# Moving the transposes of a routed-attention and MoE kernel from TensorE to the DMA crossbar

## The chip, the cores and the metric

The kernel runs on one core of a Trainium2 chip. The metric is the device time of one execution in microseconds (us), median of the timed runs. A run more than 1.5% above the fastest of its kernel is put down as slow and is left out of every ratio.

A ratio below is the mean time of one kernel's fast runs over the mean time of the fast runs of the kernel before in the same rounds on the same chip, with a 95% interval. It is therefore not quite the ratio of the medians that stand beside it.

## The reference

Four batches of eight heads, 768 tokens, head size 64. Each token of q and k is assigned to the nearest of 16 centroids of its head, a token attends only to tokens with its own centroid, and the attention output goes through a two-layer block with h·cos(h) between the layers.

```python
q_assign = argmax(einsum('bhsd,hcd->bhsc', q_n, c_n), -1)      # q_n, k_n, c_n: normalised
k_assign = argmax(einsum('bhsd,hcd->bhsc', k_n, c_n), -1)
mask = q_assign[:, :, :, None] == k_assign[:, :, None, :]
scores = where(mask, q @ k.T / sqrt(D), -1e9)
x = (softmax(scores) @ v)  ->  (3072, 512)
h = x @ w_in               # 512 -> 2048
out = (h * cos(h)) @ w_out # 2048 -> 512
```

## The kernel before

Heads are taken in pairs, sixteen pairs in all, four to a batch. For each pair, q and k are scaled and split into an fp16 high part and an fp16 low part, side by side in a staging tile `stg`. TensorE transposes the tile, the centroid matmuls and a row maximum give the one-hot assignment, and the transposed one-hots are put as 16 extra rows under the 64 rows of q and k. Then one matmul with 80 rows of depth gives score plus mask at once.

```python
stg[p] = op_pool.tile([P, 2, 2, NT, 2, D], FP16, name="stg")      # op_pool: 2 buffers
...
def tr(p, hh, a, act=False):                     # four a pair
    trp = ps_one.tile([P, NT, P], FP16, name="one")
    for t in range(NT):                          # NT = 6
        nc.tensor.transpose(out=trp[:, t, :], in_=st[:, a, hh, t]..., identity=ident)
    xT = op_pool.tile([P, S], FP16, name=f"qkT{a}{hh}", bufs=3)
    nc.vector.tensor_copy(out=xT, in_=trp...)
    qkT[p, a, hh] = xT
...
def ot(p):                                       # one-hots of the pair
    for t in range(NT):
        nc.tensor.transpose(out=tro[:, t, :], in_=oh[:, t], identity=ident)
    nc.vector.tensor_scalar(out=ohT, in0=tro..., scalar1=oh_mul, scalar2=oh_add, ...)
    for hh in range(2):
        for a in range(2):                       # to partitions 64..79 of qkT
            nc.sync.dma_start(out=qkT[p, a, hh][D:KDIM, :], in_=ohT[r0:r0 + NCL])
...
def e_chunk(p, c):                               # scores, then exp
    nc.scalar.activation(out=e_flat[...], in_=ps, func=AF.Exp, scale=1.0 / SUNIT)
...
def g_tr(p):                                     # attention output -> xt, for the MoE matmuls
    for t in range(NT):
        nc.tensor.transpose(out=trx[:, t, :], in_=st[:, t], identity=ident)
    nc.vector.tensor_copy(out=xt_of[b][:, hp, :], in_=trx...)
...
# stage s: scores of pair s, with as fillers: centroids and one-hots of s+1,
# attention-times-v and x transpose of s-1, splits and transposes of s+2, output matmuls
# SyncE issues all loads of q, k, v, the one-hot copies and the stores, in order.
```

After every fourth pair comes an MoE block (the two-layer block of the reference), which reads the transposed x of the batch. The kernel puts TensorE's results into PSUM tiles; the copy from there is called an evacuation below (63 of the 64 copies of transposed q and k are by VectorE, 551 ns each).

The softmax here doesn't subtract the row's maximum and nothing guards it: scores larger than these inputs give would overflow.

## Time and profile before

| quantity of the kernel before | value |
|---|---|
| median time | 373.2 us |
| span of the profiled run | 373.6 us |
| TensorE busy | 336.1 us, 90% |
| VectorE, ScalarE busy | 230.2 us, 210.1 us |
| traffic | 31.42 MB |
| start to the first MoE block | 96.73 us |

The prediction below shows the lines of the page and reads them. The granted clock (PEclk) is the share of full speed at which TensorE was allowed to run. The DMA share is the mean busy share of the 16 DMA engines. The run that was profiled (375.4 us) is put down as slow, 1.5% above the fastest run of this kernel on any chip of the study (369.7 us), so its stage lengths may be about 1% long.

For the sections that follow I cut every profile at the same marks: the moments at which ScalarE loads its cosine table (an MoE block begins) and its exponential table (attention begins again), ACT_TABLE_LOAD in the trace, 1.28 us each. This gives eight stages.

### The profile page before, as it was taken

Reading aid. Unit: us, or ns where it says so; the run is one execution under the profiler, and the core shown is the slowest. Engines: PE = TensorE matmul, PEld = TensorE weight load, DVE = VectorE, ACT = ScalarE, POOL = GpSimd, SP = SyncE. Lnnn points to the kernel's source line nnn. Section 1 sums busy time; section 2 is a strip of 40 time slices with the busy share of each in tenths; the row PEclk is TensorE's granted clock in tenths of the full one; section 3 lists DMA queues with packets and bytes.
Section 4 is the critical chain, followed back from the end, with each engine's and each line's share of the span. In section 5 each row is a group of like instructions: output and inputs, shape, how many; then the busy total and the mean of one; then the engine's idle time right before and its main releaser. Section 6 shows DMA issues by size and latency. Waiting matters only on the chain.

```text
span 373.6 us, 8520 instructions
## 1 busy us (share of the span) xinstructions
PE 336.1 (90%) x3656; PEld 242.6 (65%) x3656; DVE 230.2 (62%) x438; ACT 210.1 (56%) x205; POOL 28.1 (8%) x64
## 2 busy tenths in 40 slices
PE   0596569779999899999999899999998999999995
PEld 0465357566887567766977666769875666676662
DVE  5779266784765678777555767866656442354451
ACT  3163367557644677777434686786446888243320
POOL 4610021010000001100100000110000000000000
PEclk9998598895899999999999899999999999999999
DMA  7999295432420022542210110100000000101002
GB/s 230 341 241 267 77 187 150 136 104 88 147 71 28 30 80 98 145 138 78 89 44 29 36 35 12 39 31 12 2 29 30 25 29 28 58 2 56 31 28 84
DMA packets 21334, 31.42 MB, mean 84 GB/s; under 512 B 2416, under 2 KB 17712, under 8 KB 21296
## 3 DMA queue, kind: packets, MB, share of 16 engines
q1 hardware_dynamic: 18608, 26.68, 21.7%
q0 software_dynamic: 2688, 4.19, 6.3%
q8 instruction: 28, 0.46, 0.5%
q14 instruction: 10, 0.08, 0.1%
HBM read 27.30 MB, written 6.29 MB: 90 GB/s over the span
## 4 chain that ended last, share of the span: by engine, by line
PE 76%; ACT 10%; DMA 7%; DVE 4%; issue 1%; SPq 1%; ACTq 0%; DVEq 0%
PE one L316 22%; PE big L297 21%; PE big L246 16%; PE one L264 8%; ACT e_ring L252 7%; PE one L175 6%; DMA qkT<-ohT 6%; ACT cos_t L303 2%; DMA qk_nat<-in_q_dram 2%; PE one L282 2%; PE one L190 1%; ACT L252 1%; DVE g L304 1%; PE one L213 1%; DVE stg L167 1%
## 5 line engine op out<-in xcount | busy, mean ns | idle before, releaser
L252 ACT ACTIVATE e_ring<-big 128x1024 f16<-128x1024 f32 x144 | 143.1, 1023 | 62.4 <-PE big L246 61.3
L246 PE MATMUL big<-qkT,qkT 80*128 80x512 f16 (+1 forms) x384 | 96.6, 357 | 19.3 <-DMA qkT<-ohT 12.1
L303 ACT ACTIVATE cos_t<-big,bias_pi 128x1024 f16<-128x1024 f32 x48 | 53.5, 1114 | 77.1 <-PE big L297 77.0
L316 PE MATMUL one<-w_out_sb,g 128*128 128x512 f16 x384 | 96.3, 379 | 0.0
L297 PE MATMUL big<-xt,w_in_sb 128*128 128x256 f16 x768 | 92.1, 272 | 0.1
L304 DVE TENSOR_TENSOR g<-big,cos_t 128x1024 f16<-128x1024 f32 x48 | 58.7, 1223 | 52.5 <-ACT cos_t L303 52.5
L297 PEld LDWEIGHTS <-w_in_sb 128*128 128x128 f16 x768 | 74.2, 98 | 15.8 <-issue 0.2
L246 PEld LDWEIGHTS <-qkT 80*128 80x128 f16 x384 | 35.2, 104 | 43.2 <-DMA qkT<-ohT 12.6
L316 PEld LDWEIGHTS <-g 128*128 128x128 f16 x384 | 37.1, 98 | 32.9 <-issue 0.8
L264 PEld LDWEIGHTS <-e_ring 128*128 128x128 f16 x1152 | 48.2, 101 | 8.3 <-issue 2.9
L264 PE MATMUL one<-v_ext,e_ring 128*128 128x65 f16 x1152 | 51.2, 199 | 0.0
L321 DVE COPY o_sb<-one 128x512 f32<-128x512 f32 x24 | 16.6, 690 | 35.4 <-PE one L316 35.4
L155 POOL CAST v_ext<-v_nat 128x384 f16<-128x384 f32 x32 | 20.1, 637 | 222.8 <-PE one L264 169.3
L181 DVE COPY qkT<-one 128x768 f16<-128x768 f16 x63 | 32.2, 551 | 6.6 <-PE one L175 5.8
L167 DVE SCALAR_TENSOR_TENSOR stg<-qk_nat,stg 128x384 f16<-128x384 f32 x64 | 33.9, 553 | 0.1
L175 PE MATMUL one<-ident,stg 128*128 128x128 f16 x384 | 32.4, 246 | 0.0
L175 PEld LDWEIGHTS <-stg 128*128 128x128 f16 x384 | 28.8, 112 | 3.4 <-issue 1.6
L271 DVE RECIPROCAL recip<-one 128x6 f32<-128x6 f32 x32 | 6.2, 194 | 28.1 <-PE one L264 27.9
L166 DVE TENSOR_SCALAR stg<-qk_nat 128x384 f16<-128x384 f32 x64 | 21.1, 358 | 2.2 <-DMA qk_nat<-in_k_dram 1.2
L197 DVE TENSOR_REDUCE csum<-one 128x192 f32<-128x384 f32 x32 | 16.7, 552 | 6.0 <-PE one L190 5.7
L272 DVE TENSOR_TENSOR av_stage<-one,recip 128x384 f16<-128x384 f32 x32 | 17.8, 555 | 0.7
L190 PE MATMUL one<-cside,qkT 128*128 128x32 f16 x384 | 14.4, 178 | 2.2 <-DVE qkT L181 1.9
(45 smaller groups left out, 109.8 us busy)
## 6 DMA issues: line engine op xcount, KB each, us to landing
v_nat<-in_v_dram SPq DMA_DIRECT2D x16, 384.0 KB, 4.8
out_dram<-o_sb SPq DMA_DIRECT2D x24, 256.0 KB, 2.0
qk_nat<-in_q_dram SPq DMA_DIRECT2D x15, 384.0 KB, 3.4
qk_nat<-in_k_dram SPq DMA_DIRECT2D x15, 384.0 KB, 3.8
w_in_sb<-in_moe_w_in_dram POOLq DMA_DIRECT2D x4, 512.0 KB, 10.3
w_out_sb<-in_moe_w_out_dram POOLq DMA_DIRECT2D x4, 512.0 KB, 12.3
qkT<-ohT SPq DMA_DIRECT2D x60, 24.0 KB, 1.9
qk_nat<-in_q_dram SPq DMA_DIRECT2D x2, 192.0 KB, 3.0
```

The source lines that it names most:

```text
L155: nc.gpsimd.tensor_copy(out=v_bufs[(2 * p + hh) % NV][:, :, 0:D], in_=v_nat[:, hh])
L166: nc.vector.tensor_scalar_mul(dst[:, :, 0, :], src, ASCALE)
L167: nc.vector.scalar_tensor_tensor(out=dst[:, :, 1, :], in0=src, scalar=ASCALE, in1=dst[:, :, 0, :], op0=ALU.mult, op1=ALU.subtract)
L175: nc.tensor.transpose(out=trp[:, t, :], in_=st[:, a, hh, t].rearrange("p c d -> p (c d)"), identity=ident)
L181: nc.vector.tensor_copy(out=xT, in_=trp.rearrange("p t q -> p (t q)"))
L246: nc.tensor.matmul(ps[:, x:x + n], lhsT=qkT[p, 1, hh][0:KDIM, jt * P:(jt + 1) * P], rhs=qkT[p, 0, hh][0:KDIM, col:col + n], start=True, st ...
L252: nc.scalar.activation(out=e_flat[:, base + c * CW:base + (c + 1) * CW], in_=ps, func=AF.Exp, scale=1.0 / SUNIT)
L264: nc.tensor.matmul(av[:, i, :], lhsT=e_ring[:, r + j, i * P:(i + 1) * P], rhs=vx[:, j, :], start=(j == 0), stop=(j == NT - 1))
L297: nc.tensor.matmul(ps[:, fi, :], lhsT=w_in_sb[:, ft, (f0 + fi) * P:(f0 + fi + 1) * P], rhs=xt_of[b][:, ft, cols], start=(ft == 0), stop=(f ...
L303: nc.scalar.activation(out=cos_t, in_=ps, func=AF.Sin, bias=bias_pi2, scale=1.0)
L304: nc.vector.tensor_tensor(out=g[:, f0:f0 + FQ, :], in0=ps, in1=cos_t, op=ALU.mult)
L316: nc.tensor.matmul(ops, lhsT=g[:, f, i * P:(i + 1) * P], rhs=w_out_sb[:, f, :], start=(f == 0), stop=(f == NFPT - 1))
```

## The change

The intent is to take 546 transposes away from TensorE, the engine that bounds the kernel (busy 336.1 of 373.6 us), and their evacuations away from VectorE. From pair 1 on a DMA transposes the whole staging tile (`dma_start_transpose` in the program, DMA_TRANSPOSE in the traces; crossbar transpose in the texts). The one-hots are then written over the low parts of that tile, and a second crossbar transpose brings q, k and the one-hots into place together. The attention output goes through the crossbar as well. The mask's constant moves into the bias of the exponential, and the weights are loaded from the second pair on.

```diff
+    def tr_dma(p, second=False):
+        xT = op_pool.tile([P, 2, 2, NT, P], FP16, name="xT2" if second else "xT1", bufs=2)
+        nc.sync.dma_start_transpose(
+            out=xT.rearrange("p a h t q -> p (a h t) q"),
+            in_=stg[p].rearrange("p a h t c d -> p (a h t c d)"))
+        ... qkT[p, a, hh] = xT[:, a, hh]
 ...
-    def ot(p): ...
+        for a, val in ((0, 1.0), (1, GAP)):                  # in c_post, p >= 1
+            dst = stg[p][:, a, :, :, 1, 0:NCL]
+            nc.vector.tensor_tensor(out=dst, in0=cs_of[p][:, :, a], in1=..., op=ALU.is_ge)
+            if a:
+                nc.vector.tensor_scalar_mul(dst, dst, GAP)
 ...
-                             func=AF.Exp, scale=1.0 / SUNIT)
+                             func=AF.Exp, scale=1.0 / SUNIT, bias=bias_gap)
 ...                                                         # g_tr
-        for t in range(NT):
-            nc.tensor.transpose(out=trx[:, t, :], in_=st[:, t], identity=ident)
-        nc.vector.tensor_copy(out=xt_of[b][:, hp, :], in_=trx...)
+        nc.sync.dma_start_transpose(out=xt_of[b][:, hp].rearrange("p (t q) -> p t q", t=NT), in_=st)
 ...
-        r.append((34, lambda hh=hh, a=a: tr(p, hh, a)))       # tr_list
+        r = [(8, lambda hh=hh, a=a: split(p, hh, a)) for hh in range(2) for a in range(2)]
+        return r + [(1, lambda: tr_dma(p))]
 ...
-        return [(34, lambda: ot(p))]
+        return [(1, lambda: tr_dma(p, True))]
 ...
-                if weight_jobs:
+                if s >= 1 and weight_jobs:
```

More of the change, by code (lines that the diff above doesn't have):

```diff
@@ L76 @@
     bias_pi2 = consts.tile([P, 1], FP32, name="bias_pi2")
-    oh_mul = consts.tile([P, 1], FP32, name="oh_mul")
-    oh_add = consts.tile([P, 1], FP32, name="oh_add")
+    bias_gap = consts.tile([P, 1], FP32, name="bias_gap")
     warm = consts.tile([1, 1], FP32, name="warm")
-    NV, NOH = 8, 2
+    NV = 8
     v_bufs = [consts.tile([P, NT, DE], FP16, name=f"v_ext{i}") for i in range(NV)]
-    oh_bufs = [consts.tile([P, NT, 2, 2, 2 * NCL], FP16, name=f"oh{i}") for i in range(NOH)]
+    oh_buf = consts.tile([P, NT, 2, 2, 2 * NCL], FP16, name="oh")
     NE = 4
@@ L176, in tr @@
                                 identity=ident)
-        xT = op_pool.tile([P, S], FP16, name=f"qkT{a}{hh}", bufs=3)
+        xT = op_pool.tile([P, S], FP16, name=f"qkT{a}{hh}", bufs=1)
         if act:
@@ L182, in tr @@
         qkT[p, a, hh] = xT
+    def tr_dma(p, second=False):
[3 more added lines that the diff above has]
+            in_=stg[p].rearrange("p a h t c d -> p (a h t c d)"))
+        for a in range(2):
+            for hh in range(2):
+                qkT[p, a, hh] = xT[:, a, hh].rearrange("p t q -> p (t q)")
     def c_mm(p, hh, a):
@@ L204, in c_post @@
         nc.vector.reduce_max(out=r, in_=cs, axis=AX.X)
-        oh = oh_bufs[p % NOH].rearrange("p t h a c -> p (h a) t c")
-        nc.vector.tensor_tensor(out=oh[:, 2 * h0:2 * (h0 + n), :, 0:NCL], in0=cs,
-                                in1=r.to_broadcast([P, 2 * n, NT, NCL]), op=ALU.is_ge)
-    def ot(p):
-        oh = oh_bufs[p % NOH].rearrange("p t h a c -> p t (h a c)")
-        tro = ps_one.tile([P, NT, P], FP16, name="one")
-        for t in range(NT):
-            nc.tensor.transpose(out=tro[:, t, :], in_=oh[:, t], identity=ident)
-        ohT = small_pool.tile([P, S], FP16, name="ohT")
-        nc.vector.tensor_scalar(out=ohT, in0=tro.rearrange("p t q -> p (t q)"),
-                                scalar1=oh_mul, scalar2=oh_add, op0=ALU.mult, op1=ALU.add)
-        for hh in range(2):
-            for a in range(2):
-                r0 = (2 * hh + a) * 2 * NCL
-                nc.sync.dma_start(out=qkT[p, a, hh][D:KDIM, :], in_=ohT[r0:r0 + NCL])
+        if p == 0:
+            oh = oh_buf.rearrange("p t h a c -> p (h a) t c")
+            nc.vector.tensor_tensor(out=oh[:, 2 * h0:2 * (h0 + n), :, 0:NCL], in0=cs,
+                                    in1=r.to_broadcast([P, 2 * n, NT, NCL]), op=ALU.is_ge)
+            return
+        for a, val in ((0, 1.0), (1, GAP)):
+            dst = stg[p][:, a, :, :, 1, 0:NCL]
+            nc.vector.tensor_tensor(
+                out=dst, in0=cs_of[p][:, :, a],
+                in1=r.rearrange("p (h a) t o -> p h a t o", a=2)[:, :, a].to_broadcast([P, 2, NT, NCL]),
+                op=ALU.is_ge)
+            if a:
+                nc.vector.tensor_scalar_mul(dst, dst, GAP)
     def ot_head(p, hh):
-        oh = oh_bufs[p % NOH].rearrange("p t h a c -> p t h (a c)")
+        oh = oh_buf.rearrange("p t h a c -> p t h (a c)")
         n = 4 * NCL
@@ L230, in ot_head @@
         if hh == 0:
-            nc.scalar.mul(qkT[p, 0, hh][D:KDIM, :], tf[0:NCL], -GAP)
+            nc.scalar.copy(qkT[p, 0, hh][D:KDIM, :], tf[0:NCL])
         else:
-            nc.vector.tensor_scalar_mul(qkT[p, 0, hh][D:KDIM, :], tf[0:NCL], -GAP)
-        nc.vector.tensor_scalar(out=qkT[p, 1, hh][D:KDIM, :], in0=tf[2 * NCL:3 * NCL],
-                                scalar1=-1.0, scalar2=1.0, op0=ALU.mult, op1=ALU.add)
+            nc.vector.tensor_copy(out=qkT[p, 0, hh][D:KDIM, :], in_=tf[0:NCL])
+        nc.vector.tensor_scalar_mul(qkT[p, 1, hh][D:KDIM, :], tf[2 * NCL:3 * NCL], GAP)
     def e_chunk(p, c):
@@ L278, in g_tr @@
             xt_of[b] = xt_pool.tile([P, HPB, S], FP16, name="xt")
-        trx = ps_one.tile([P, NT, P], FP16, name="one")
-        st = av_of.pop(p).rearrange("p t h d -> p t (h d)")
-        for t in range(NT):
-            nc.tensor.transpose(out=trx[:, t, :], in_=st[:, t], identity=ident)
-        nc.vector.tensor_copy(out=xt_of[b][:, hp, :], in_=trx.rearrange("p t q -> p (t q)"))
+        st = av_of.pop(p).rearrange("p t h d -> p (t h d)")
+        nc.sync.dma_start_transpose(out=xt_of[b][:, hp].rearrange("p (t q) -> p t q", t=NT), in_=st)
     g_of = {}
@@ L328, in g_list @@
     def g_list(p):
-        return [(34, lambda: g_tr(p))]
+        return [(1, lambda: g_tr(p))]
     def tr_list(p):
-        r = []
-        for hh in range(2):
-            for a in range(2):
-                r.append((0, lambda hh=hh, a=a: split(p, hh, a)))
-                r.append((34, lambda hh=hh, a=a: tr(p, hh, a)))
-        return r
+        r = [(8, lambda hh=hh, a=a: split(p, hh, a)) for hh in range(2) for a in range(2)]
+        return r + [(1, lambda: tr_dma(p))]
     def c_list(p):
@@ L381 @@
         nc.vector.memset(bias_pi2, PI_HALF)
-        nc.gpsimd.memset(oh_bufs[0], 0.0)
-        for hh in range(2):
-            for a in range(2):
-                r0 = (2 * hh + a) * 2 * NCL
-                nc.gpsimd.memset(oh_mul[r0:r0 + 2 * NCL], (-GAP, -1.0)[a])
-                nc.gpsimd.memset(oh_add[r0:r0 + 2 * NCL], (0.0, 1.0)[a])
-        nc.gpsimd.memset(oh_bufs[1], 0.0)
+        nc.vector.memset(bias_gap, -GAP / SUNIT)
+        nc.gpsimd.memset(oh_buf, 0.0)
         for t in v_bufs:
@@ L391 @@
         centroids_prep(cn_raw)
-        nc.scalar.activation(out=warm, in_=oh_add[0:1], func=AF.Exp)
+        nc.scalar.activation(out=warm, in_=bias_pi2[0:1], func=AF.Exp)
         def head0(hh):
```

## The prediction

Its 56 ns are those of a 128x128 transpose on TensorE: one lasts 246 ns in the mean, but the chain has 24 of them in 1.34 us. Its rivals assume about 3, 5 and 10 us for one transpose by the DMA; these were assumptions, and no run had shown such a transpose yet. With 2.25 of them (two, and a quarter for x) and 1.3 us of loads a pair they come to about 8, 13 and 24 us of SyncE.

> **What bounds the kernel now.** I read the page's busy shares and slices first, then busy time by stretch, then the chain that ended last, then the waits and the issue rows. Page of the kernel before (engine busy us, then tenths in 40 slices):
>
> ```profile
> PE 336.1 (90%) x3656; PEld 242.6 (65%) x3656; DVE 230.2 (62%) x438; ACT 210.1 (56%) x205; POOL 28.1 (8%) x64
> ...
> PE   0596569779999899999999899999998999999995
> ...
> PEclk9998598895899999999999899999999999999999
> DMA  7999295432420022542210110100000000101002
> ```
>
> TensorE is full from about slice 10 on; before that it has holes, its clock drops, and the DMA engines are busy instead. The same by stretches (us, busy us with counts, granted clock, DMA share, GB/s); I cut at the first score matmul, at the starts of pair 1 and of the first MoE matmuls, and at the start of each later MoE block:
>
> ```profile
> 18.25:41.44 23.19, 16.04 (x165) 11.62 (x166) 16.37 (x36) 8.67 (x9) 2.14 (x4) 0.84 1.00 239
> 41.44:95.94 54.50, 46.77 (x573) 34.44 (x573) 35.38 (x86) 34.76 (x36) 7.68 (x10) 0.78 0.46 122
> 95.94:176.40 80.46, 78.44 (x918) 57.41 (x916) 59.54 (x115) 53.06 (x52) 4.24 (x8) 1.00 0.27 86
> 176.40:254.70 78.30, 76.38 (x898) 56.85 (x897) 53.52 (x97) 51.23 (x50) 4.24 (x8) 0.98 0.12 41
> ```
>
> So there are two regimes. From 96 us TensorE is the bound: 78.4 of 80.5 us, ScalarE 53, VectorE 60. Before 96 us pairs 1 to 4 take 54.5 us, 13.6 us each, at a granted clock of 0.78, though ScalarE needs only 8.7 us for each. The chain and the waits say why:
>
> ```profile
> 33.26 8.13 DMA qkT<-ohT
> ...
> 50.33 5.86 DMA qkT<-ohT
> ...
> 65.54 4.02 DMA qkT<-ohT
> ...
> 80.04 3.67 DMA qkT<-ohT
> ```
>
> ```profile
> PE big L246 <- DMA qkT<-ohT: 12.1, 4, 5.6
> ```
>
> The chain holds 21.7 us of the four one-hot copies that move the transposed mask rows into qkT. The first took 8.13 us for 24 KB a copy beside a DMA share of 1.00: it sat behind loads. TensorE idled 12.1 us for them[...].
>
> [...] the chain has 24 of them in 1.34 us, 56 ns each, and that is what removal returns. [...] The loads here moved 26.68 MB in 21.7% of 373.6 us, 329 GB/s of engine time. [...] SyncE's copy issues here take 0.37 to 0.47 us. [...]
>
> **The change, part by part.**
>
> TensorE loses, for pairs 1 to 15, 24 q/k transposes and 6 of one-hots each, and 6 of x for all 16 pairs: 360 + 90 + 96 = 546. After 95.94 us the trace holds 220 + 60 + 72 = 352 of them: 352 x 0.056 = 19.7 us, all on the bound. Another 144 lie in 41 to 96 us at clock 0.78: 144 x 0.072 = 10 us, but there the DMA wait, not TensorE, ends the stage.
>
> VectorE loses per pair four evacuations of 0.551, one of 0.672 (ohT), one of 0.555 (xt) and one compare of 0.557: 3.99 us. It gains two compares on half the elements (0.40 each, by the 128x192 compare of pair 0) and one multiply (estimate 0.35): 1.2 us. Net -2.8 x 15 = -42 us, none of it on a bound, but it makes the split and compare chains shorter.
>
> ScalarE: a bias on the exponential, no change.
>
> DMA: each of pairs 1 to 15 now moves its whole staging tile, 128 x 3,072 fp16 = 768 KB, twice, and each pair 192 KB of x: 30 x 768 + 16 x 192 KB = 26.7 MB more on 31.4. [...] Four copies of ohT (2.41 us of SyncE) go away per pair.
>
> [...] per steady pair it then issues two transposes, one x transpose (a quarter of one) and three loads (1.3 us). [...]
>
> The steady pair takes 12.67 us now (score waits at 142.91, 155.59 and 168.26 us) and would need 12.67 - 36 x 0.056 = 10.65 of TensorE.
>
> The early pairs: the chain is split, transpose, centroid matmuls, sums and compares (about 3.5 us of VectorE), second transpose, scores. The scheduler splits two pairs ahead, so the first transpose can hide. The second replaces the ohT copy in the same place, but starts earlier (no TensorE transpose or evacuation before it, 1.2 us)[...]. The weights moved out of the first pair's stage take 2 MB fp32 of traffic away from where the DMA share is 1.00.
>
> The end: the last x transpose is 0.34 us of TensorE plus 0.55 of VectorE; [...] exposed once at the end and in part at three block starts: +2 to +5 us.
>
> **Rivals.**
>
> A, the transposes are cheap (about 3 us each, issue included). Steady -19.7; pairs 1 to 4 drop from 13.6 to about 11.2 us, -10; stage 0 -2; block starts and end +5: 373 - 27 = 346. For: [...] shares of 0.12 to 0.27 in the steady part leave room.
>
> B, SyncE's issue or the crossbar at about 5 us per transpose becomes the pace of the attention stages: 12.8 us where TensorE needs 10.65 and the old pair took 12.67. Only the MoE blocks (about 31 us, few transposes) let it catch up by one transpose: 5 us a block, about -10 in all; the early pairs stay near 13.6 us with the second transpose exposed in place of ohT; +5 at block starts: about 368. For: the 12.1 us of waits on a far smaller DMA, and SyncE's in-order waits (outputs waiting for VectorE already hold it 155.7 us in all), which would hold a transpose back.
>
> C, about 10 us per transpose: 24 us a pair, 15 x 24 = 360 plus about 60 of head and tail: near 420. [...] Against: a tuned kernel would hardly have kept it.
>
> D, the transposes are fast but the second one is exposed at each early pair with a slow clock: A without the 10 us, about 356.
>
> **Range and chances.** I give A and D together 0.5, B 0.35, C 0.15. The 2% edges are 365.8 and 380.7. A and D lie below, B straddles the lower edge (a quarter below, half within, a quarter above), C above. That gives about 0.56 faster, 0.18 within, 0.26 slower. The point lies between D and B, 358 us; 340 to 395 leaves out the best tenth and most of C.
>
> **What would show it.** The distance of the scores' starts in the steady stages: 10.7 us for A, 12.7 and more for B, with TensorE waiting for the transposed tile and the share of SyncE busy issuing. The issue row of the transposes: landing about 5 us (A), 7 (B), 12 or more (C). The stretch from 41 to 96 us: 45 us (A), 54 (B, D). VectorE's busy time should fall by about 42 us to 188, and TensorE's instructions by 546; both hold whatever the time does. The prediction is wrong if transposes queued behind loads take far longer than alone, if the last pair's x transpose costs over 5 us, or if TensorE's granted clock, 1.00 in the steady part, falls there [...].

## The result, and the profile after

The changed kernel is correct and slower: 397.2 us median of four runs (394.09 to 403.81), against 373.21 us. The ratio of the fast runs is 1.0615, interval 1.051 to 1.0721. The profiled run is a fast one with a span of 392.0 us.

The page of the kernel after: busy us of each engine, then three lines in tenths of 40 slices, then the packets.

```profile
PE 312.8 (80%) x3110; PEld 211.1 (54%) x3110; DVE 189.5 (48%) x378; ACT 216.4 (55%) x205; POOL 25.3 (6%) x55
...
PE   0590363763959999799299999797899999999995
...
PEclk9999985995889999999889999899699999999999
DMA  7899999999996017999993036989500181101002
...
DMA packets 125329, 56.61 MB, mean 144 GB/s; under 512 B 107376, under 2 KB 121712, under 8 KB 125296
```

The work did go away: 546 fewer TensorE instructions and 40.7 us less of VectorE. But the DMA line now stands at 9 from slice 3 to slice 12, again from 17 to 21, and at 8 or 9 from 26 to 28, and TensorE's holes, with most of its lower clock digits, lie in and just behind these stretches. Before, the DMA line was at 5 or less from slice 7 on. Of the 125,329 packets now 107,376 are under 512 bytes.

The eight stages (lengths in us, each the distance between two loads of a ScalarE table in the trace):

| stage | before | after | difference |
|---|---|---|---|
| start, pairs 0 to 4 | 96.73 | 106.38 | +9.65 |
| MoE block 1 | 30.44 | 35.05 | +4.61 |
| attention 1 | 49.05 | 46.03 | -3.02 |
| MoE block 2 | 31.17 | 39.97 | +8.80 |
| attention 2 | 47.77 | 43.85 | -3.92 |
| MoE block 3 | 30.56 | 36.17 | +5.61 |
| attention 3 | 33.08 | 29.06 | -4.02 |
| last MoE block and end | 54.80 | 55.49 | +0.69 |
| sum | 373.60 | 392.00 | +18.40 |

So the change does give 11 us in the later attention stages. It loses 19 us in the three inner MoE blocks and 10 us before the first. The stretches themselves: window, length, busy us (instructions) of PE, PEld, DVE, ACT and POOL, then granted clock, DMA share (packet times may overlap, so it can pass 1) and GB/s. First the kernel before, attention 1 and MoE block 2:

```profile
127.17:176.22 49.05, 47.08 (x610) 32.26 (x608) 39.65 (x88) 37.46 (x37) 3.22 (x6) 1.00 0.34 103
176.22:207.39 31.17, 31.12 (x308) 24.92 (x306) 16.89 (x19) 14.65 (x13) 1.02 (x2) 1.00 0.17 57
```

Then the kernel after: pairs 1 to 4 and the wait that follows, and the same two stages.

```profile
41.40:105.39 63.99, 38.02 (x503) 25.37 (x504) 27.53 (x72) 36.36 (x36) 7.45 (x12) 0.79 1.12 225
...
141.43:187.46 46.03, 42.15 (x474) 26.12 (x472) 26.39 (x65) 39.01 (x38) 3.29 (x6) 0.96 0.91 186
187.46:227.43 39.97, 32.48 (x298) 25.48 (x298) 19.30 (x26) 14.64 (x14) 1.02 (x2) 0.91 0.55 123
```

In 41 to 105 us the DMA share is 1.12, and yet the engines move only 225 GB/s, and TensorE works 38 of 64 us. In attention 1 the DMA share has gone from 0.34 to 0.91. In MoE block 2 TensorE has 7.5 us of holes (39.97 less 32.48) where it had none.

Part of the chain that ended last in the kernel after (start, us, what):

```profile
13.81 10.07 DMA xT<-stg
...
33.58 12.31 SPq L186
...
79.75 17.14 DMA xT<-stg x2
...
187.10 2.87 SPq L186
190.69 4.16 DMA xt<-av_stage
```

The one-hot copies of the chain before are replaced by crossbar transposes (10.07 us for one, 17.14 us for two). L186 is the issue of a transpose by SyncE: one issue held the queue for 12.31 us. The last two lines are the start of MoE block 2: the small x transpose stands behind a q/k transpose in SyncE's order, and TensorE waits for both.

The waits of TensorE and of VectorE in the kernel after (us in total, times, longest):

```profile
PE one L199 <- DMA xT<-stg: 26.2, 5, 15.5
PE big L300 <- DMA xt<-av_stage: 15.0, 4, 7.5
PE big L252 <- DMA xT<-stg: 12.0, 5, 6.2
```

```profile
DVE stg L165 <- DMA xT<-stg: 52.6, 11, 9.0
```

TensorE waits 53 us for transposes, where it waited 12.1 us for one-hot copies before. The fourth line is one that the prediction did not have at all. L165 is the first write of a split into the staging tile. VectorE stands there until the crossbar transpose that reads the tile's former contents is done. Before, TensorE read that tile, and VectorE never waited for that.

The issue rows of the kernel after (count, median us to landing):

```profile
xT<-stg SPq DMA_TRANSPOSE x30, 6.6
...
xt<-av_stage SPq DMA_TRANSPOSE x16, 2.8
```

One q/k transpose ran with nothing beside it, between 279 and 286 us. This window's DMA share and rate, in 40 slices of 0.17 us:

```profile
DMA  0000000599999999999999999999810000000006
GB/s 0 0 0 0 0 0 0 116 223 226 215 206 209 212 226 212 214 217 218 215 227 220 212 217 215 217 215 188 178 26 0 0 0 0 0 0 0 0 0 161
```

For 3.6 us the DMA engines are full (0.9 or more in 20 slices; a share of 1.12 over 280.5 to 284.1 us), at about 216 GB/s. So this one transpose, alone, filled all sixteen engines. With 2.25 of them a pair (two whole ones and a quarter), 2.25 x 3.6 = 8.1 us of all engines; the loads of a pair (3 x 384 KB, at the 329 GB/s worked out in the prediction) take about 3.6 us more, so about 11.7 us a pair, against the 10.65 us that TensorE would need (an estimate from these durations).

### The profile page after: what moved, and what is told of

Same layout as the page of the kernel before. It is cut to its first block, busy times and chain, and to the rows that moved or that the text cites. A ratio compares the mean times of both kernels' runs of the same rounds, so it can differ in the third digit from the quotient of the medians.

```text
span 392.0 us, 7311 instructions
## 1 busy us (share of the span) xinstructions
PE 312.8 (80%) x3110; PEld 211.1 (54%) x3110; DVE 189.5 (48%) x378; ACT 216.4 (55%) x205; POOL 25.3 (6%) x55
## 2 busy tenths in 40 slices
DMA packets 125329, 56.61 MB, mean 144 GB/s; under 512 B 107376, under 2 KB 121712, under 8 KB 125296
## 4 chain that ended last, share of the span: by engine, by line
PE 57%; DMA 26%; SPq 7%; DVE 6%; ACT 3%; issue 1%; ACTq 0%
PE big L300 20%; DMA xT<-stg 20%; PE one L319 16%; PE big L252 11%; PE one L270 7%; SPq L186 6%; DMA xt<-av_stage 4%; DMA qk_nat<-in_q_dram 2%; DVE g L307 2%; PE one L199 2%; ACT cos_t L306 2%; DVE stg L166 1%; DVE stg L165 1%; ACT e_ring L258 1%; SPq L111 1%
## 5 line engine op out<-in xcount | busy, mean ns | idle before, releaser
L258 ACT ACTIVATE e_ring<-big,bias_gap 128x1024 f16<-128x1024 f32 x144 | 149.4, 1138 | 54.9 <-PE big L252 54.0
L300 PE MATMUL big<-xt,w_in_sb 128*128 128x256 f16 x768 | 96.9, 282 | 16.3 <-DMA xt<-av_stage 15.0
L252 PE MATMUL big<-xT 80*128 80x512 f16 (+1 forms) x360 | 85.9, 344 | 16.1 <-DMA xT<-stg 12.0
L300 PEld LDWEIGHTS <-w_in_sb 128*128 128x128 f16 x768 | 77.3, 101 | 36.7 <-issue 18.3
L252 PEld LDWEIGHTS <-xT 80*128 80x128 f16 x360 | 33.2, 100 | 43.9 <-DMA xT<-stg 14.2
L270 PEld LDWEIGHTS <-e_ring 128*128 128x128 f16 x1152 | 50.9, 103 | 10.6 <-issue 1.1
L165 DVE TENSOR_SCALAR stg<-qk_nat 128x384 f16<-128x384 f32 x64 | 21.8, 370 | 56.0 <-DMA xT<-stg 52.6
L199 PE MATMUL one<-cside,xT 128*128 128x32 f16 x360 | 12.6, 180 | 28.3 <-DMA xT<-stg 26.2
L199 PEld LDWEIGHTS <-xT 128*128 128x128 f16 x360 | 11.8, 98 | 33.2 <-DMA xT<-stg 31.4
L222 DVE TENSOR_TENSOR stg<-csum,rmax 128x192 f16<-128x192 f32 x30 | 10.0, 374 | 0.7 <-DVE recip L277 0.3
L252 PE MATMUL big<-qkT,qkT 80*128 80x512 f16 (+1 forms) x24 | 9.0, 512 | 1.0 <-ACT e_ring L258 0.7
```

The source lines that it names most:

```text
L165: nc.vector.tensor_scalar_mul(dst[:, :, 0, :], src, ASCALE)
L199: nc.tensor.matmul(cs[:, a, t].rearrange("p i c -> p (i c)"), lhsT=qkT[p, a, hh][:, t * P:(t + 1) * P], rhs=cside[:, h].rearrange("p i c - ...
L252: nc.tensor.matmul(ps[:, x:x + n], lhsT=qkT[p, 1, hh][0:KDIM, jt * P:(jt + 1) * P], rhs=qkT[p, 0, hh][0:KDIM, col:col + n], start=True, st ...
L258: nc.scalar.activation(out=e_flat[:, base + c * CW:base + (c + 1) * CW], in_=ps, func=AF.Exp, scale=1.0 / SUNIT, bias=bias_gap)
L270: nc.tensor.matmul(av[:, i, :], lhsT=e_ring[:, r + j, i * P:(i + 1) * P], rhs=vx[:, j, :], start=(j == 0), stop=(j == NT - 1))
L300: nc.tensor.matmul(ps[:, fi, :], lhsT=w_in_sb[:, ft, (f0 + fi) * P:(f0 + fi + 1) * P], rhs=xt_of[b][:, ft, cols], start=(ft == 0), stop=(f ...
```

## The experiments

All gave a correct result. Unless it says otherwise, a difference is against the 397.2 us of the kernel after. That kernel was run once more, as `after_again`, to see how far two rounds lie apart: 395.86 us, ratio 1.0577 (1.0451 to 1.0703).

> The changed kernel once more, beside the three below on the same chip: 394 to 400 us, ratio 1.05 to 1.07.

For the start of the first MoE block the expectations use another mark than the text: its first unbroken run of matmuls, 95.9 us in the kernel before and 111.0 us after. The text uses the load of the cosine table, 96.73 and 106.38 us.

### Where the early 10 us come from

**late_only.** Pairs 1 to 4 keep the old way (TensorE transposes, one-hot copies); from pair 5 on the kernel is the changed one.

```diff
+    PE_FIRST = lambda p: p < 5
+    OH_OLD = lambda p: p < 5
 ...
+        if PE_FIRST(p):            # tr_list: split and tr, as before
+        if OH_OLD(p):              # ot_list: ot, as before
```

> The changed kernel with pairs 1 to 4 made the old way (TensorE transposes, small copies); from pair 5 on by the crossbar. Early theory (15 us of the 18.4 us lost are lost before the first MoE block): its start falls from 111.0 to 95 to 99 us and the total to 380 to 385 us. Rival (the loss is a property of every pair and the early part only shows it first): the later blocks lose what the early part gains, total 390 us or more.

Measured: 381.75 us, ratio 1.0256 (1.02 to 1.0312). The first MoE block starts at 91.30 us in place of 106.38. So taking the crossbar work of pairs 1 to 4 away gives back 15 us, all before the first MoE block. That is more than the 9.65 us that the kernel after lost there: late_only is 5.4 us ahead of the kernel before, and all of it is gained before the scores of pair 1. The first score matmuls of pair 1 in the kernel before, then in late_only (in brackets the idle time before them and what ended it):

```profile
41.44 1.89 PE L246 MATMUL big<-qkT,qkT 80*128 80x512 f16 x5 [5.59 <-DMA qkT<-ohT]
```

```profile
35.94 1.04 PE L276 MATMUL big<-xT 80*128 80x512 f16 x5 [0.51 <-DMA xT<-ohT]
```

From there to the MoE block both take the same time, 55.3 and 55.4 us. The later start of the weights is the likeliest reason for the 5.4 us, but late_only differs in buffers too, and no run puts the later start alone into the kernel before.

**before_plus_idle.** The kernel before, computing all it did, with both crossbar transposes of each pair added into tiles that nobody reads. To make room, the one-hots and ohT have one buffer instead of two, so a part of the effect could be theirs.

```diff
+    def tr_dma(p, second=False):
+        xT = op_pool.tile([P, 2, 2, NT, P], FP16, name="xT2" if second else "xT1", bufs=1)
+        nc.sync.dma_start_transpose(out=xT..., in_=stg[p]...)
 ...
-        return r
+        return r + [(1, lambda: tr_dma(p))]
-        return [(34, lambda: ot(p))]
+        return [(34, lambda: ot(p)), (1, lambda: tr_dma(p, True))]
```

> The kernel before, unchanged in its dependences, with both crossbar transposes of each pair issued beside it into tiles that nobody reads (one-hot buffer and ohT single, to make room). Fullness theory (the traffic itself delays loads and copies): the start of the first MoE block moves from 95.9 to 105 us or later, total 385 to 395 us, ratio 1.03 to 1.06. Latency theory (only waiting for a transpose's result costs): nothing waits for them, time 371 to 377 us, ratio 1.00 to 1.01.

Measured: 402.69 us, ratio 1.0795 (1.0729 to 1.0862), slower than the kernel after. The early stage in its profile, same columns as above:

```profile
41.44:114.10 72.66, 44.41 (x568) 32.66 (x565) 36.57 (x84) 34.81 (x36) 4.83 (x8) 0.77 1.10 175
```

The DMA share goes from 0.46 in the kernel before to 1.10, and the stretch from 54.50 to 72.66 us, although no result of these transposes is used. So waiting for a transpose's result is not needed to stretch the early stage: the loads and the 24 KB one-hot copies come later beside the added transposes (in the median of the run a load of k lands in 4.5 us, against 3.8, and a copy in 2.9, against 1.9; TensorE waits 24.4 us for the copies, against 12.1). VectorE waited for the staging tile only 2.3 us in this stretch, so that is not the reason here. What the run does not separate is full DMA engines from SyncE's queue: the chain that ended last has 4% of the span in SyncE's issue of transposes, and the loads and copies stand in the same queue.

**weights_first.** In the kernel after, the weights are loaded from the first pair on, as before.

```diff
-                if s >= 1 and weight_jobs:
+                if weight_jobs:
```

> The changed kernel with the weight loads from the first pair on, as before. If deferring them helped as meant (DMA is full at the start): 2 to 5 us slower than after, 400 us. If it only moved the same traffic within a stretch that is full anyway (14 to 111 us): within 2 us of after, 397 us.

Measured: 396.79 us, ratio 1.0614 (1.0503 to 1.0726). In the kernel after, the later start of the weights is worth nothing that these runs can show, in either direction. Where the early pairs go the old way it may be worth more (late_only above).

**one_transpose** and **one_transpose3.** Halve the crossbar work: one transpose a pair, and the one-hots by TensorE and small copies as before. The first version gave the transposed tile two buffers.

```diff
+    OH_OLD = lambda p: True
 ...                                            # one_transpose3 besides
-        xT = op_pool.tile([...], name="xT2" if second else "xT1", bufs=2)
+        xT = op_pool.tile([...], name="xT2" if second else "xT1", bufs=3)
```

> The changed kernel with only the first q/k transpose by the crossbar; one-hots transposed by TensorE and copied as four small DMAs, as before. This takes 768 KB of crossbar traffic from each pair, 3.6 us of all 16 engines. Fullness theory (the DMA engines are full from 14 to 111 us and set the pace there): the start of the first MoE block, 111.0 us in after, falls to 95 to 101 us, and the total to about 383 us. Rival (what counts is that a DMA of a fixed latency stands in the chain of each pair, however little it moves): four small copies stand there in its place, the start of the block stays at 106 us or later, total 392 us or more.

Measured: 424.76 us, ratio 1.14 (1.1345 to 1.1455), the worst but one of all. This was a flawed experiment: the tile now lives from the first transpose through the scores and two buffers are one too few, so that a transpose can have to wait for the scores of the pair two before it. The waits of VectorE for the staging tile rose to 72.2 us.

> one_transpose with three buffers for the transposed tile in place of two: there it was held from the transpose until the end of the pair's scores, so the transpose of two pairs ahead could not start; the three buffers are what before had. Buffer theory: the 424.8 us of one_transpose were this shortage, and it falls to 380 to 388 us. Fixed-latency theory (a small DMA in the chain costs as much as a large one, and two kinds of DMA together more): stays over 400 us.

Measured with three buffers: 388.04 us, ratio 1.0395 (1.0308 to 1.0482); the first MoE block starts at 95.85 us. Taking away half of the crossbar traffic gives back 9 us. In the profiles the early part is 10.5 us shorter and the rest 5.3 us longer; the old one-hot copies bring their own waits (16.9 us) with them.

**loads_on_pool.** If the order of SyncE's queue is what holds the transposes back, then loads issued by another engine should free it.

```diff
-                nc.sync.dma_start(out=qk_nat[...], in_=x[b, hs]...)
+                (nc.sync if p < 2 else nc.gpsimd).dma_start(out=qk_nat[...], in_=x[b, hs]...)
 ...                                            # and v_nat likewise
```

> The changed kernel with the q, k and v loads of pairs 2 to 15 issued by GpSimd in place of SyncE. Fullness theory (the 16 DMA engines are full until 111 us, whoever issues): within 4 us of after, 393 to 401 us. Queue theory (SyncE in order is what delays: a load waits behind a transpose that is still being issued or waited for): the early part shortens by 5 us or more, 385 to 391 us.

Measured: 441.6 us (434.9 to 443.96), three of four runs slow, so no ratio is given. All expectations missed. In its profile (a slow run) the centroid matmuls wait far longer for the first transpose:

```profile
PE one L199 <- DMA xT<-stg: 81.0, 6, 23.3
```

The loads land in 5.8 to 9.9 us (medians; 4.0 to 5.9 us in the kernel after), while four transposes, with their waits, took SyncE's queue from 14.14 to 78.94 us. My reading was that the transposes starve beside the loads of a second queue; it rests on a slow run alone and is not shown. That the kernel got slower holds for its one fast run too (434.9 us).

**after_c_late.** The centroid matmuls, which wait for the first transpose, are emitted after the attention-times-v matmuls of the stage, so that TensorE has other work in the meantime.

```diff
-            if s + 1 < NPAIR:
-                fill += c_list(s + 1)
             ... f_list(s - 1)
             if s + 1 < NPAIR:
+                fill += c_list(s + 1)
                 fill += ot_list(s + 1)
```

> The changed kernel with the centroid matmuls of the next pair emitted after the attention-value matmuls of the last one, so that the first transpose has some 2.5 us more and the second less. If the loss in the steady pairs is TensorE waiting at the centroid matmuls for the first transpose: 5 us or more faster, 385 to 391 us. If both transposes are short of time alike (their sum is the stage): the wait moves to the scores, 393 to 402 us.

Measured: 402.76 us, ratio 1.0794 (1.0741 to 1.0847). A miss: the wait moves from the centroid matmuls (21.6 us in place of 26.2) to the score matmuls (27.1 in place of 12.0), as the second transpose then starts later. Moving the wait did not shorten the stage.

### The MoE block starts

**x_on_pe.** Only the x transposes go back to TensorE.

```diff
-        nc.sync.dma_start_transpose(out=xt_of[b][:, hp]..., in_=st)
+        for t in range(NT):
+            nc.tensor.transpose(out=trx[:, t, :], in_=st[:, t], identity=ident)
+        nc.vector.tensor_copy(out=xt_of[b][:, hp, :], in_=trx...)
```

> The changed kernel with the x transposes back on TensorE. Theory 1 (the waits for the x transposes at the four block starts, 15.0 us in the profile of after, are a loss of their own): those waits go, 96 transposes of 0.056 us come back (+5.4 us), so about 9 us faster than after: 388 us, ratio to before about 1.04. Rival (the x waits only stand in for something else, such as late q/k transposes): the waits move to other lines and the time stays at 394 to 400 us.

Measured: 390.28 us, ratio 1.048 (1.0416 to 1.0544), 7 us better by the medians, though its interval touches that of the kernel after. The three inner MoE blocks fall from 111.2 us together to 101.4 us; the waits for xt fall from 15.0 us to 5.2 us. The attention stages behind them take most of it back (126.1 us together, against 118.9): there TensorE has its x transposes again, 5.4 us of work in the whole kernel by the expectation's figure.

### The bias

**no_bias.** The constant is put into the one-hot rows of k (GAP times one-hot, minus GAP), and the exponential takes no bias tile.

```diff
-                nc.vector.tensor_scalar_mul(dst, dst, GAP)
+                nc.vector.tensor_scalar(out=dst, in0=dst, scalar1=GAP, scalar2=-GAP, ...)
 ...
-                             func=AF.Exp, scale=1.0 / SUNIT, bias=bias_gap)
+                             func=AF.Exp, scale=1.0 / SUNIT)
```

> The changed kernel with the gap taken off in the k rows (GAP*one-hot - GAP, same instructions on VectorE) in place of a bias operand on the exponential. In after 9 exponentials in a row took 9.35 us against 5 in 4.70 us before, 0.10 us more each. If ScalarE's pace counts only in the one early pair that it bounds (49.5 to 58.9 us), 1 to 2 us faster than after: 395 us. If it counts in all attention stages, 144 x 0.1 = 14 us: 383 us.

Measured: 391.13 us, ratio 1.0469 (1.0381 to 1.0558); weights_first at 396.79 us, so 5.7 us better by the medians (4.7 against after_again), with intervals that overlap. The exponential of the kernel after and of the kernel before, with the least, median and greatest duration in ns:

```profile
L258 ACT ACTIVATE e_ring<-big,bias_gap x144: 1106/1115/1240, 19.3 to 335.4; 128x1024 f16<-128x1024 f32 x144
```

```profile
L252 ACT ACTIVATE e_ring<-big x144: 1017/1024/1042, 19.3 to 317.8; 128x1024 f16<-128x1024 f32 x144
```

The bias tile costs 91 ns on each of 144 exponentials, 13 us summed over them, and no_bias is back at 1025 ns; this is shown. ScalarE is busy 216.4 us in the kernel after and 206.4 us in no_bias. What the tile costs the whole kernel is not shown: in the profile of no_bias the attention stages, where the exponentials are, are no shorter (121.1 us together, against 118.9), and MoE block 2 is (35.6 against 40.0). The prediction had "no change": I had looked at the added transposes and not at the added operand.

### All three together

**late_mix.** late_only, x_on_pe and no_bias in one kernel (the diffs above).

> Pairs 1 to 4 the old way, x on TensorE, no bias; q/k and one-hots by the crossbar from pair 5 on. If the parts add up (early part -15, x waits -9, bias -2 against 397): about 371 us, near or a little under before's 373. If the steady part's TensorE saving of 220+60 transposes x 0.056 = 15.7 us also shows once the waits are gone: 358 to 363 us. If steady pairs wait for the crossbar instead: 375 to 385 us.

Measured: 374.17 us, ratio 1.0036 (0.9958 to 1.0114): level with the kernel before. Taken one by one the three gave 15.4, 6.9 and 5.7 us by the medians, 28 together; combined they give 23. And TensorE still has the 30 transposes a pair less for pairs 5 to 15, with nothing to show for it. In its profile VectorE waits 36.7 us for the crossbar to release the staging tile.

### Better than both

**before_direct.** If the one-hot copies are the trouble of the kernel before, they can go without a crossbar: VectorE writes the transposed one-hots from PSUM straight to partitions 64 to 79 of qkT, in four small instructions in place of one large.

```diff
-        ohT = small_pool.tile([P, S], FP16, name="ohT")
-        nc.vector.tensor_scalar(out=ohT, in0=tro..., scalar1=oh_mul, scalar2=oh_add, ...)
+        tf = tro.rearrange("p t q -> p (t q)")
 ...
-                nc.sync.dma_start(out=qkT[p, a, hh][D:KDIM, :], in_=ohT[r0:r0 + NCL])
+                nc.vector.tensor_scalar(out=qkT[p, a, hh][D:KDIM, :], in0=tf[r0:r0 + NCL],
+                                        scalar1=(-GAP, -1.0)[a], scalar2=(0.0, 1.0)[a], ...)
```

> The kernel before with the one-hot rows written by VectorE from PSUM straight into qkT (four instructions on 16 partitions, about 0.55 us each by the pair-0 ones, 2.2 in place of 0.67 us), no ohT and no small copies. The 12.1 us of TensorE waits for those copies and the lowered clock in pairs 1 to 4 should go: the first MoE block starts at 83 to 88 us instead of 95.9, total 360 to 365 us, ratio about 0.97. If the early part is bound by the loads instead, 370 to 374 us.

Measured: 362.2 us, ratio 0.9736 (0.9656 to 0.9815), faster than both kernels, though the interval does not clear 2%. The first MoE block starts at 79.23 us in place of 96.73, TensorE is busy 91% of the span, and the waits for one-hots are gone. The later stages of its profile are 8 us longer than before (284.8 against 276.9 us from the first MoE block to the end), but the profiled run, 365.75 us, was the slowest of four of which the others took 361.6 to 362.2 us. VectorE now works 46.1 of the 51.4 us of attention 1, and TensorE waits for it here and there (2.7 us for g, 2.2 for qkT and 1.7 for av_stage in the whole run).

**direct_late.** before_direct plus one crossbar transpose a pair for q and k from pair 5 on, where the DMA engines have room (shares of 0.27 and 0.12 from 96 to 255 us in the kernel before); the one-hots stay on TensorE and VectorE.

```diff
+        if p >= 5:                               # tr_list
+            r = [(8, lambda hh=hh, a=a: split(p, hh, a)) for hh in range(2) for a in range(2)]
+            return r + [(1, lambda: tr_dma(p))]
```

> before_direct (362.2 us; one-hot rows written by VectorE) with one crossbar transpose a pair from pair 5 on in place of the 24 on TensorE; its result is needed a pair later. Engine time a pair of the DMA: 3.6 transpose + 3.6 loads = 7.2 of about 11 us, so not full. If the crossbar then hides: 11 pairs x 24 x 0.056 = 14.8 us less on TensorE, 347 to 351 us. If about half of it comes back as waits: 354 to 358 us. If a crossbar transpose always costs its pair more than it saves: 363 us or more.

Measured: 370.47 us, ratio 0.9962 (0.9876 to 1.0049). Taking 24 transposes and four evacuations from each of eleven pairs made it slower by 8 us. TensorE waits 12.3 us at the x transposes for the attention output, which VectorE delivers late; VectorE itself waits 14.0 us for the staging tile.

**direct_late_g**, with its control **before_direct_g.** The x transposes are emitted after the stage's output matmuls, so that TensorE does not stand at them. The control does the same without any crossbar.

```diff
-            if s >= 1 and not after_s:
-                fill += g_list(s - 1)
             ... moe2_list ...
+            if s >= 1 and not after_s:
+                fill += g_list(s - 1)
```

> direct_late (370.5 us) with the x transposes of a pair emitted after the stage's MoE matmuls instead of right after the pair's attention-value matmuls. Order theory (TensorE in order waits about 2 us a pair for av_stage because the q/k transposes that used to run meanwhile are gone): those 12.3 us go, 356 to 360 us, and below before_direct's 362. If the saved work cannot be used for another reason (clock, ScalarE, x late for the MoE blocks): 366 us or more.

> Control: before_direct (362.2 us) with the same move of the x transposes. There the q/k transposes of TensorE fill the gap, so by the order theory it gains nothing: 360 to 366 us. If it gains as much as direct_late_g (10 us), the crossbar has no part in that gain.

Measured: 364.71 us, ratio 0.9769 (0.9715 to 0.9823), between its two expectations, and for the control 367.32 us, ratio 0.9833 (0.9807 to 0.9859). So the move gains 6 us where the crossbar has taken the transposes and gains nothing without it (0.9736 before it); but with the crossbar the kernel is not clearly faster than the control, as their intervals overlap. In the one place where nothing stopped it a pair takes 10.96 us between its centroid matmuls (121.43 to 132.39 us). But VectorE waits 21.5 us for the staging tile, one wait of 7.0 us in MoE block 2, behind which TensorE waits 4.6 us for VectorE; that block grows to 40.12 us (31.17 in before_direct).

```profile
DVE stg L167 <- DMA xT<-stg: 21.5, 7, 7.0
```

**direct_all_g.** As direct_late_g, with the crossbar from pair 1 on.

```diff
-        if p >= 5:
+        if p >= 1:
```

> direct_late_g with the crossbar for the q/k transposes of pairs 1 to 4 too (one a pair; one-hots by VectorE). Fullness theory: the early part now has 3.6 us of crossbar beside 3.6 of loads and about 6 of weights a pair, about 13 us in stages of 12 us or so: the first MoE block starts 8 us or more later than in direct_late_g, 365 to 372 us. If one transpose a pair is affordable there: within 4 us of direct_late_g.

Measured: 382.3 us, ratio 1.024 (1.0198 to 1.0283). Even a single transpose a pair costs 18 us when it stands among the early loads: the first MoE block starts at 93.58 us in place of 78.87, and TensorE waits 20.5 us for the transposed tile.

### The staging tile

The theory by now: the crossbar holds the staging tile until its transpose has landed; VectorE, in order, stands at the next split (21.5 us in direct_late_g); what is queued behind the split on VectorE (attention output, g, evacuations) comes late to TensorE, which idles and then runs at a lower clock. The rival: the wait is only where slack shows, and the DMA engines set the pace. A third staging buffer tells them apart.

```diff
-            stg[p] = op_pool.tile([P, 2, 2, NT, 2, D], FP16, name="stg")
+            stg[p] = op_pool.tile([P, 2, 2, NT, 2, D], FP16, name="stg", bufs=3)
```

**direct_late_g_stg3** is direct_late_g with this line alone.

> direct_late_g with three staging buffers in place of two. Theory (the crossbar holds the staging tile, VectorE waits in order at the next split, and TensorE then waits for VectorE and slows): VectorE's 21.5 us of waits at the split for the transpose go to under 5 us, the pairs from 5 on take about 11 us each, granted clock 0.97 or more, and the time falls from 364.7 to about 352 to 358 us, ratio to before 0.945 to 0.96. Rival (the wait at the split is only where the pair's slack shows; the late landing of the transposes or the DMA engines themselves set the pace): the wait moves to the centroid or score matmuls, which then wait for the transposed tile, and the time stays within 2 us of 364.7, ratio 0.972 to 0.982.

Measured: 357.8 us (355.37 to 359.15), ratio 0.9567 (0.9513 to 0.9621), the fastest kernel; its interval lies below that of direct_late_g. VectorE's waits fall only from 21.5 to 14.0 us, not to the expected under 5:

```profile
DVE stg L167 <- DMA xT<-stg: 14.0, 5, 5.1
```

The time fell where the waits went: MoE block 2 from 40.12 to 33.80 us and attention 2 from 43.64 to 40.77 us, while attention 1, where 10.8 of the 14.0 us remain, grew from 48.82 to 53.33 us. Attention 2 now runs as the prediction had wished. These are its centroid matmuls (start, us, engine, line, tile):

```profile
195.80 0.76 PE L202 MATMUL one<-cside,xT 128*128 128x32 f16 x24
206.01 0.76 PE L202 MATMUL one<-cside,xT 128*128 128x32 f16 x24
216.97 0.76 PE L202 MATMUL one<-cside,xT 128*128 128x32 f16 x24
227.94 0.46 PE L202 MATMUL one<-cside,xT 128*128 128x32 f16 x12
```

The distances are 10.2, 11.0 and 11.0 us. (This kernel takes only 24 of the prediction's 36 transposes from a pair; 12.67 less 24 x 0.056 would be 11.3 us.) Attention 1 does not run so, because there a wait remained even with three buffers. VectorE's split after its longest wait, and TensorE's next work that waited on VectorE (in brackets the idle time and what ended it):

```profile
142.28 0.36 DVE L167 TENSOR_SCALAR stg<-qk_nat 128x384 f16<-128x384 f32 x1 [5.14 <-DMA xT<-stg]
```

```profile
145.18 0.51 PE L294 MATMUL one<-ident,av_stage 128*128 128x128 f16 x6 [1.61 <-DVE av_stage L284]
```

and the three stretches of 5 us around it (columns as above):

```profile
138.00:143.00 5.00, 5.00 (x33) 2.66 (x31) 0.72 (x2) 4.31 (x6) 0.23 (x1) 1.00 0.95 230
143.00:148.00 5.00, 2.50 (x38) 1.49 (x36) 4.88 (x13) 1.79 (x2) 0.00 (x0) 1.00 0.21 73
148.00:153.00 5.00, 3.71 (x51) 2.95 (x50) 4.30 (x11) 1.63 (x3) 0.20 (x1) 0.61 0.66 151
```

These three lines show the order of events. In the first VectorE does 0.72 us of work, because it stands at the staging tile (the wait of 5.14 us) while the DMA share is 0.95. In the second VectorE catches up (4.88 us) and TensorE works only 2.50 of the 5 us, at a granted clock of 1.00. In the third TensorE's clock is 0.61, and in the next 5 us it is 0.70. So here the clock fell after the idle time and did not cause it. The longest single hole before that was 1.61 us; how much idling is enough no run here shows.

**after_stg3** is the kernel after with the same line. Room was made by letting pair 0 use a buffer of the second transposes' ring.

```diff
-        xT = op_pool.tile([P, S], FP16, name=f"qkT{a}{hh}", bufs=1)
+        if p not in xT_of:
+            xT_of[p] = op_pool.tile([P, 2, 2, NT, P], FP16, name="xT2", bufs=2)
+        xT = xT_of[p][:, a, hh].rearrange("p t q -> p (t q)")
```

> The kernel after with three staging buffers in place of two (room made by letting pair 0 use a buffer of the ring of the second transposes). Theory: VectorE's 52.6 us at the split go to under 15 us; the pairs of the later attention stages come closer to TensorE's 10.65 us; the early pairs stay bound by the crowded DMA engines; so about 380 to 388 us, ratio to before 1.02 to 1.04. Rival (DMA engines full at two whole transposes a pair, 11.8 us of all 16 per pair): the wait moves to the centroid and score matmuls, 392 to 400 us, ratio 1.05 to 1.07.

Measured: 388.36 us, ratio 1.0405 (1.0362 to 1.0449), 9 us better than the kernel after and just above what the theory gave. VectorE's waits for the crossbar fall from 52.6 to 33.4 us, not to under 15, and its waits for the loads of q grow from 1.1 to 17.4 us:

```profile
DVE stg L166 <- DMA xT<-stg: 33.4, 6, 9.3
...
DVE stg L166 <- DMA qk_nat<-in_q_dram: 17.4, 6, 7.7
```

Its attention 1 got longer (50.0 us against 46.0), attention 2 too (46.2 against 43.9), while the early stage and MoE blocks 2 and 3 got shorter. So the third staging buffer was worth about 2% in each of the two kernels (in this one pair 0's buffers differ as well). That the full DMA engines are the next limit with two whole transposes a pair fits the DMA share of 0.92 that attention 1 keeps, but no run shows it by itself.

## Why the prediction was wrong

**What bounds the kernel: right.** TensorE from the first MoE block on, and the one-hot copies before it. before_direct shows the second by taking the copies away: 11 us in the whole, 17.5 us before the first MoE block.

**The counts: right.** TensorE lost exactly 546 instructions; VectorE went from 230.2 to 189.5 us, where "about 42 us to 188" was predicted. The two compares took 0.37 us each (0.40 predicted) and the multiply 0.205 us (0.35).

**"352 x 0.056 = 19.7 us, all on the bound": this is the step that failed first.** It is right that TensorE's need fell: a pair of direct_late_g_stg3, with 24 of the 36 transposes gone, takes 11.0 us where a pair took 12.67 us before. But the kernel after received only 11 us of it in the attention stages and lost 19 in the three inner MoE blocks. The step treated the stages as bound by one engine which only needed less work. It looked at what the transposes deliver to, and not at what they hold or stand behind. Two things came in its place. First, 14.8 of the 19 us are TensorE's waits for x at the starts of those blocks, where the x transpose stands behind the q/k transposes in SyncE's queue; x_on_pe shows these. Second, VectorE waits with the next split into the staging tile until the crossbar transpose that reads it is done (52.6 us in 11 waits), and what follows on VectorE waits with it. In the kernel after, TensorE's other waits are for the q/k transposes themselves (38 us); in the direct_late kernels, where this could be followed, they are for VectorE, and TensorE's clock is lower behind the holes (0.61 behind the one that was followed, in direct_late_g_stg3). The third staging buffer shows that this was so, for about 2%.

**"Shares of 0.12 to 0.27 in the steady part leave room": wrong.** These shares were averages over attention stages and MoE blocks together. Most of the transposes fall into the attention stages, and there the DMA share became 0.91 and 0.81. The 3 us a transpose of rival A were assumed; alone on the engines it took 3.6 us, at 216 GB/s, and it filled all engines (share 1.12). Landing, "about 5 us (A)", was 5.4 us alone, 6.6 us in the median and 10.1 us for the first one, beside which loads ran.

**SyncE's issue "at about 5 us per transpose" (rival B): too long when alone, too short in company.** An issue took 3.57 us at best and 12.31 us at worst. Alone it lasted as long as the engines were full (3.6 us), so in these runs it was no constant. Rival B was nearest in picture, SyncE's issue or the crossbar at the pace, with a time of 368; it lacked the loss in the early part and the held staging tile.

**"Pairs 1 to 4 drop from 13.6 to about 11.2 us, -10": wrong in sign.** The stretch before the first MoE block grew by 9.65 us. It is the stage whose DMA share was already 0.46 to 1.00, and the change put eleven transposes of 768 KB into it (two each of pairs 1 to 5 and one of pair 6). The prediction named this as what would make it wrong ("if transposes queued behind loads take far longer than alone") and yet gave it no rival of its own. before_plus_idle, late_only and direct_all_g show that the crossbar work costs this stage its time; whether by full DMA engines or by the held queue of SyncE stays open.

**"Block starts and end +5": mis-sized.** TensorE waited 15.0 us for x: 3.0, 7.5, 4.3 and 0.2 us. A single x transpose lands in 2.8 us in the median, but it stands behind a transpose of q and k in the same queue, whose issue alone takes 3.9 us in the median. The end, for which most of the term was meant, cost 0.2 us. x_on_pe gives back 7 us in all.

**"ScalarE: a bias on the exponential, no change": wrong for the instruction.** 91 ns each, 13 us summed. For the whole kernel the medians say 5.7 us, within overlapping intervals.

**The weights: no effect in the kernel after.** "Stage 0 -2" was not to be seen in weights_first. In late_only, where the early pairs go the old way, 5.4 us were gained before pair 1's scores.

**Range and chances.** 397.2 us lies just above the upper end of 395. The shares also add up to 0.59, 0.17 and 0.24 and not to 0.56, 0.18 and 0.26, a small slip. Chance went to cheap transposes because each rival spoke of the duration of one transpose, or of average shares, and none of all transposes together with the loads of one stage.

What stays open: whether full DMA engines or SyncE's queue stretch the early stage; why attention 1 and 2 grew in after_stg3, and attention 1 in direct_late_g_stg3; why the later stages of before_plus_idle also grew (its buffers differ as well); and whether late_mix with a third staging buffer would have come below the kernel before. The fastest kernel gained nothing in the later part over the kernel before by its profile (280.1 us against 276.9 us from the first MoE block to the end); its gain is the early 20.7 us. It is 4.4 us faster than before_direct by the medians, and the intervals do not overlap. That this is the crossbar's gain is not fully shown: before_direct with a third staging buffer was not run, though its VectorE never waited for a reader of the staging tile, so there is little that the buffer alone could give.

## What to carry to other kernels

Before moving work from the bounding engine to the DMA, add up the DMA time of the stage into which it falls, loads and copies included, not the average of the kernel; and leave alone the stage in which loads already set the pace. Ask of every moved operation which buffer it holds, for how long and who must write that buffer next: here, where the crossbar read the staging tile in TensorE's place, one buffer more was worth about 2%. And where a small copy is what the critical stage waits for, look first whether an engine can write the place directly; that took 11 us here with no transfer at all, and the crossbar paid only after it, in the stages with room, with a third buffer.
